# Three last stores of a filter-and-MLP kernel go through GpSimd's queue instead of SyncE's

## The chip, the cores and the metric

The kernel runs on one core of a Trainium2 chip. Its time is in device microseconds (us), taken over whole executions. One further execution was recorded by the hardware profiler, and its trace is what is read below. The engines are called PE (TensorE, matrix products), DVE (VectorE), ACT (ScalarE), POOL (GpSimd) and SP (SyncE). SP, ACT and POOL issue DMAs, each in the order of its own instruction queue.

## What is computed

The input `x` has 8 sequences of 3008 tokens with 256 features, in float32. Each feature is filtered along its sequence in the frequency domain, and then every token goes through two dense layers with a leaky ReLU between them:

```python
X = np.fft.rfft(x, axis=1)
Y = X * (filt_r + 1j * filt_i)[None, :, :]
y = np.fft.irfft(Y, n=3008, axis=1).reshape(8 * 3008, 256)
h = y @ w_in                       # 256 -> 2048
out = np.maximum(0.01 * h, h) @ w_out   # 2048 -> 256, float32
```

## The kernel before

The transform is done as small matrix products over 94 x 32 = 3008 positions, sequence by sequence. Its stages move data through DMAs on SP and end in `yt`, the filtered tokens. The last of POOL's work for it is the sum in L326 for the eighth sequence.

The dense layers run over 47 chunks of 512 tokens (`ci` = 0 to 46). For chunk `ci`, `moe1` (L516) multiplies by `w_in` into PSUM, and ACT writes the leaky ReLU into `gts[ci]` (L527). One chunk later the product with `w_out` follows. From chunk 3 on, it is made of seven half-size products, with sums on DVE before them (L563) and after them (L625 to L681). A chunk's result lies in two tiles, `rows(ci, 0)` and `rows(ci, 1)`, of two groups of 128 tokens each. `store` (L581) and `pieces` (L569) cut a group of 128 tokens into one or more DMAs, because output rows of different sub-sequences do not lie at one stride.

All steps are put on one list with a time (`at`, `soon`) and are emitted in the order of those times. So a delay given to `soon` only decides the place of an instruction in its engine's queue, and at run time each instruction waits for semaphores alone. Each DMA uses one of eight semaphores of its kind in turn, one set of eight for SP and ACT together and one for POOL.

After chunk 46's first layer, PE has only the products of chunk 46 left. They end in this order, each followed by its DVE instruction and its stores:

- `m2` (L639): DVE adds the left 128 columns of two token groups into `rows(46, 0)` (L641). These are the early half-width tiles, two DMAs of 128 tokens x 128 columns, through `store` (L583).
- the product with `wt[3]`, in two tiles, in `m4_tile` (L669): DVE writes L670 for each token group. The largest piece of group 0 is stored by SP and that of group 1 by ACT (L673). What is left of group 1, eight tokens of full width, is the leftover piece (L675).
- the last product, in two tiles, in `m3_tile` (L677): DVE writes L678, and the right 128 columns of each group are stored, group 0 by SP and group 1 by ACT (L583).

Behind its last instruction every engine has the program's end (all on L808): SP waits for every DMA semaphore in turn, each engine has a DRAIN, and POOL then waits until the others have reported, gives them leave, drains and clears semaphores, and a second such round ends the program.

Of the kernel before, what the change touches and what calls it, by code (L numbers as in the profile page):

```python
# [11 lines left out]
P = 128  # L12
# [65 lines left out]
def kernel(  # L78
# [9 lines left out]
    nc = tc.nc  # L88
# [83 lines left out]
    def at(time, f):  # L172
        clock["n"] += 1
        heapq.heappush(work, (time, clock["n"], f))
# [12 lines left out]
    def soon(delay, f):  # L187
        at(clock["now"] + delay, f)
# [356 lines left out]
    def sum_places(ci):  # L545
        return last_sums if ci == NCHUNK - 1 else [s1, quarter(ci, 1, 0), s2, s4]
# [8 lines left out]
    def quarter(ci, i, j):  # L555
        return gts[ci][:, ts(j, NCH), ts(token_half(ci, i), TH)]
# [12 lines left out]
    def pieces(ci, tj, of, d0=0, dn=D):  # L569

        t, end = ci * CH + tj * P, ci * CH + (tj + 1) * P
        lo = 0
        while t < end:
            e = min(end, (t // QT + 1) * QT)
            b, h = divmod(t // QT, N2 // 4)
            row = b * N + (t % QT) // 4 * N2 + 4 * h
            yield (bass.AP(tensor=out.tensor, offset=out.offset + row * D + d0,
                           ap=[[N2 * D, (e - t) // 4], [D, 4], [1, dn]]), of[lo : lo + e - t])
            lo, t = lo + e - t, e

    def store(*what, queue=nc.sync):  # L581
        for to, of in pieces(*what):
            queue.dma_start(to, of)  # L583

    def product(ci, a, w, after, last_sum=None, of=None, each=None):

        po = of
        if of is None:
            po = out_banks[done["products"] % 2][:, 0]
            done["products"] += 1  # L590
        if each is None:
            of = [po[:, t] for t in range(2)]

        def one(t, c):
            if last_sum is not None:
                need(("sum", ci, last_sum))
            nc.tensor.matmul(of[t], a()[:, c, ts(t, P)], w[:, c, :],  # L597
                             start=(c == 0), stop=(c == NCH - 1))
            if c < NCH - 1:
                return  # L600
            if each is not None:
                each(t, of[t])
            elif t == 1:
                after(po)
        return [lambda t=t, c=c: one(t, c) for t in range(2) for c in range(NCH)]

    def rows(ci, i):

        if (ci, i) not in osts:
            osts[ci, i] = outp.tile([P, 2, 3, P], FP32, tag="ost", name=f"ost_c{ci}_h{i}")  # L610
        return osts[ci, i]

    def stores(ci, i, of=range(2)):
        for j in of:
            store(ci, 2 * i + j, rows(ci, i)[:, j, 0:2, :].rearrange("p k d -> p (k d)"))

    def twice(po):
        ap = [list(v) for v in po.ap]
        return bass.AP(tensor=po.tensor, offset=po.offset, ap=[ap[0], ap[1], [0, 2], ap[2]])
# [3 lines left out]
    def last_product(ci):  # L623
        def after(po):
            add(rows(ci, 0)[:, :, 1], po, rows(ci, 1)[:, :, 2], AL.add)  # L625
            soon(AFTER[5], lambda: stores(ci, 0))
        return product(ci, lambda: sum_places(ci)[3], b22, after, 3)

    def products(ci):
        a11, a12, a21, a22 = (lambda i=i, j=j: quarter(ci, i, j) for i in range(2) for j in range(2))  # L630

        def after5(po):
            add(rows(ci, 1)[:, :, 1:3], twice(po), part[1], AL.add)
            soon(AFTER[5], lambda: stores(ci, 1))

        def m1():
            return product(ci, a11, b11, lambda po: nc.scalar.copy(t1, po))

        def m2(early=None):  # L639
            def after(po):  # L640
                add(rows(ci, 0)[:, :, 0], po, t1, AL.add)  # L641
                if early is not None:
                    soon(0.3, lambda: [store(ci, 2 + t, rows(ci, 0)[:, t, 0], 0, P) for t in range(2)])
            return product(ci, a12, b21, after)

        def m7():
            return product(ci, lambda: sum_places(ci)[1], wt[2], lambda po: add(v7, po, t1, AL.add), 1)

        def m6(of=None):
            return product(ci, lambda: sum_places(ci)[2], wt[1], lambda po: add(part[1], twice(po), part[0], AL.add), 2, of)  # L650

        if ci == NCHUNK - 1:
            free = [w[:, :CH].rearrange("p (a t d) -> p a t d", a=2, t=2)[:, 0] for w in wide + single]
            return last_product(ci - 1) + m1() + m7() + m2(ci) + m6(free[0]) + last_three(ci, free[1:])
        if ci > W0:
            items = m1() + last_product(ci - 1) + m2() + m7()
        else:
            done["products"] += 1
            items = m1() + [lambda: None] * (2 * NCH) + m2() + m7()
        items += m6()  # L660
        items += product(ci, a22, wt[3], lambda po: add(rows(ci, 1)[:, :, 0], po, u3, AL.add))
        return items + product(ci, lambda: sum_places(ci)[0], wt[0], after5, 0)

    def last_three(ci, free):

        free += [b[:, 0] for b in out_banks]
        low, high = rows(ci, 0), rows(ci, 1)

        def m4_tile(t, po):  # L669
            add(high[:, t, 0], po, u3[:, t], AL.add)  # L670
            parts = list(pieces(ci, t, high[:, t, 0:2, :].rearrange("p k d -> p (k d)")))
            parts.sort(key=lambda v: -v[1].shape[0])
            soon(0.02, lambda: (nc.sync, nc.scalar)[t].dma_start(*parts[0]))  # L673
            for v in parts[1:]:
                soon(0.6, lambda v=v: nc.sync.dma_start(*v))  # L675

        def m3_tile(t, po):  # L677
            add(low[:, t, 1], po, high[:, t, 2], AL.add)  # L678
            soon(0.02, lambda: store(ci, 2 + t, low[:, t, 1], P, P, queue=(nc.sync, nc.scalar)[t]))

        items = product(ci, lambda: sum_places(ci)[0], wt[0], lambda po: add(high[:, :, 1:3], twice(po), part[1], AL.add), 0, free[0])  # L681
        items += product(ci, lambda: quarter(ci, 1, 1), wt[3], None, of=[f[:, 0] for f in free[1:3]], each=m4_tile)
        return items + product(ci, lambda: sum_places(ci)[3], b22, None, 3, of=[f[:, 0] for f in free[3:5]], each=m3_tile)
# [63 lines left out]
    queue = [(time, n, *v) for n, (time, *v) in enumerate(groups)]  # L747
    heapq.heapify(queue)
    while queue:
        time, n, stage, b, g, f = heapq.heappop(queue)  # L750
        t = max(time, last + GAP)
# [61 lines left out]
```

## Time and profile before

| what | value |
|---|---|
| median of 3 runs (lowest to highest) | 745.34 us (744.58 to 745.47) |
| the profiled execution's own time | 744.82 us |
| its span, first to last instruction | 742.8 us |
| PE busy | 735.8 us (99%) |
| ACT busy | 559.8 us (75%) |
| DVE busy | 506.7 us (68%) |
| POOL busy | 167.6 us (23%) |
| start of POOL's last sum (L326) | 612.2 us |
| start of the last DVE instruction (L678) | 738.55 us |

The span is what the profiler sees between the first and the last instruction, and the execution's own time is 2.02 us more. Busy time of an engine is the time in which it works on an instruction. Issuing a DMA from SP or ACT, waiting for semaphores and draining are not counted as busy, so the program's end after 738.85 us shows only in single rows of the trace.

### The profile page before, as it was taken

How to read it: one execution, taken by the hardware profiler on the slowest of the kernel's cores; microseconds unless marked ns; L12 is line 12 of the kernel's file. 1: busy time of each engine (PE TensorE's matmuls, PEld its weight loads, DVE VectorE, ACT ScalarE, POOL GpSimd, SP SyncE). 2: the span in 40 equal slices, each digit the busy share in tenths (PEclk: the TensorE clock that was granted, in tenths of full speed). 3: DMA queues.
4: the chain of work that ended last, by engine and by line, in shares of the span. 5: the costliest groups of instructions: out<-in, count | busy, mean ns of one | idle time of the engine just before them, and what ended most of it. 6: DMA issues, size and time to landing. Idle time of an engine off the chain costs nothing.

```text
span 742.8 us, 18986 instructions
## 1 busy us (share of the span) xinstructions
PE 735.8 (99%) x7793; PEld 513.7 (69%) x7793; DVE 506.7 (68%) x690; ACT 559.8 (75%) x769; POOL 167.6 (23%) x171
## 2 busy tenths in 40 slices
PE   9999999999999999999999999999999999999997
PEld 3656667776777777777777777777777777777776
DVE  7987647776776766766777667766677676465566
ACT  4776797888878788877787787887777777777762
POOL 5503422332323212131232322121212210000000
PEclk9999999999999999999999999999999999999999
DMA  9997797888876666665676656544453343211012
GB/s 206 229 227 193 201 227 222 198 208 207 215 182 149 159 188 176 161 150 159 195 175 155 160 156 175 157 140 111 143 170 110 107 107 97 62 54 55 30 45 71
DMA packets 119879, 113.84 MB, mean 153 GB/s; under 512 B 16384, under 2 KB 93056, under 8 KB 119600
## 3 DMA queue, kind: packets, MB, share of 16 engines
q1 hardware_dynamic: 104457, 94.94, 43.9%
q0 software_dynamic: 15056, 17.50, 15.7%
q8 instruction: 61, 1.00, 0.6%
q10 hardware_dynamic: 279, 0.19, 0.1%
q14 instruction: 26, 0.21, 0.1%
HBM read 57.74 MB, written 50.33 MB: 145 GB/s over the span
## 4 chain that ended last, share of the span: by engine, by line
PE 98%; DVE 1%; ACT 0%; issue 0%; DVEq 0%; ACTq 0%
PE ph L524 44%; PE pf L597 18%; PE po_ps L597 18%; PE pf L262 3%; PE pf L358 3%; PE pf L311 2%; PE pf L333 2%; PE po_ps L380 2%; PE pf L689 1%; PE po_ps L689 1%; PE pf L432 0%; ACT yt L347 0%; PE pf L449 0%; PE ph L408 0%; DVE big L291 0%; DVE big L441 0%
## 5 line engine op out<-in xcount | busy, mean ns | idle before, releaser
L527 ACT ACTIVATE gt_c<-ph 128x1024 f16<-128x1024 f32 x376 | 385.6, 1026 | 131.6 <-PE ph L524 121.2
L524 PE MATMUL ph<-yt,w_in_sb 128*128 128x512 f16 x1504 | 446.9, 379 | 0.2 <-ACT yt L347 0.2
L597 PEld LDWEIGHTS <-gt_c 128*128 128x128 f16 x2800 | 203.3, 98 | 102.3
L326 POOL TENSOR_TENSOR y_b_g<-p_b_g,p_b_g 128x512 f16<-128x512 f32 x84 | 117.8, 1405 | 411.0 <-DMA p_b_g<-p_b_g 219.9
L597 PEld LDWEIGHTS <-big 128*128 128x128 f16 x2128 | 152.0, 98 | 69.2
L524 PEld LDWEIGHTS <-w_in_sb 128*128 128x128 f16 x1504 | 119.8, 98 | 12.9 <-DVE yt L347 0.4
L320 DVE TENSOR_TENSOR p_b_g<-pf,fb_sb 128x512 f32<-128x512 f32 x78 | 53.7, 688 | 31.4 <-PE pf L311 16.5
L597 PE MATMUL po_ps<-wt_sb,gt_c 128*128 128x128 f16 x704 | 70.0, 219 | 0.0
L597 PE MATMUL pf<-wt_sb,gt_c 128*128 128x128 f16 x688 | 68.5, 219 | 0.0
L597 PE MATMUL pf<-w_out_sb,gt_c 128*128 128x128 f16 x720 | 67.9, 219 | 0.0
L597 PE MATMUL pf<-wt_sb,big 128*128 128x128 f16 x704 | 67.2, 219 | 0.0
L597 PE MATMUL po_ps<-w_out_sb,gt_c 128*128 128x128 f16 x688 | 66.0, 219 | 0.0
L265 ACT CAST big<-pf 128x512 f16<-128x512 f32 x98 | 57.1, 588 | 11.7 <-PE pf L262 10.4
L597 PE MATMUL po_ps<-wt_sb,big 128*128 128x128 f16 x688 | 65.4, 219 | 0.0
L347 ACT CAST yt<-pf 128x376 f16<-128x376 f32 (+7 forms) x134 | 57.1, 441 | 10.0 <-PE pf L358 7.5
L563 DVE TENSOR_TENSOR big<-gt_c 128x2048 f16<-128x2048 f16 (+1 forms) x46 | 57.3, 1247 | 0.1
L323 DVE TENSOR_TENSOR p_b_g<-pf,fa_sb 128x512 f32<-128x512 f32 x84 | 57.2, 681 | 0.2
L563 DVE TENSOR_TENSOR big<-gt_c,big 128x2048 f16<-128x2048 f16 (+1 forms) x45 | 56.7, 1261 | 0.0
L563 DVE TENSOR_TENSOR gt_c<-gt_c 128x2048 f16<-128x2048 f16 x43 | 55.9, 1301 | 1.0
L563 DVE TENSOR_TENSOR big<-big,gt_c 128x2048 f16<-128x2048 f16 (+1 forms) x45 | 54.8, 1219 | 0.1
L335 ACT CAST big<-pf 128x512 f16<-128x512 f32 x84 | 49.0, 584 | 4.7 <-PE pf L333 2.7
L262 PE MATMUL pf<-x_sb,small_sb 128*128 128x512 f16 x109 | 41.3, 379 | 0.0
(98 smaller groups left out, 628.3 us busy)
## 6 DMA issues: line engine op xcount, KB each, us to landing
dz<-big SPq DMA_DIRECT2D x98, 256.0 KB
p_b_g<-p_b_g SPq DMA_DIRECT2D x156, 128.0 KB
out_dram<-ost_c_h SPq DMA_DIRECT2D x118, 128.0 KB
big<-dz SPq DMA_DIRECT2D x42, 256.0 KB
big<-dz SPq DMA_DIRECT2D x56, 192.0 KB
x_sb<-in_x_dram POOLq DMA_DIRECT2D x40, 192.0 KB, 4.4
x_sb<-in_x_dram POOLq DMA_DIRECT2D x2, 768.0 KB, 9.2
w_in_sb<-in_moe_w_in_dram POOLq DMA_DIRECT2D x1, 1024.0 KB, 13.7
```

The costliest lines, as they stand in the source:

```text
L262: nc.tensor.matmul(ps, fwd1, x_sb[:, ds(2 * g, 2), :], start=True, stop=True)
L265: copy(st[:, ds(2 * (g % 2), 2), :], ps)
L320: nc.vector.tensor_tensor(p2[:], ps, fb, AL.mult)
L323: nc.vector.tensor_tensor(p1[:], ps, fa, AL.mult)
L326: ("y", b, g), lambda: nc.gpsimd.tensor_tensor(y1[:], p1[:], p3[:], AL.add)))
L335: nc.scalar.copy(st2[h % 4][:, ds(2 * (g % 2), 2), :], ps)
L347: copy(yt[:, dt, ds(to, 4 * n)].rearrange("p (a c) -> p a c", c=4), v[:, ds(a, n)])
L358: nc.tensor.matmul(ps[:, j, :], z2[h % 4][:, j, ts(dt, P)], i1_sb[:, 4 * h + j, :N1], start=True, stop=True)
L524: nc.tensor.matmul(ph[:, j, :], w_in_sb[:, dt, ts(ct, P)], yt[:, dt, ds(ci * CH % RING, CH)], start=(dt == 0), stop=(dt == NDT - 1))
L527: nc.scalar.activation(gts[ci][:, ds(2 * g, 2), :], ph, AF.Lrelu)
L563: nc.vector.tensor_tensor(*(v[:, ds(c0, n)] for v in (o, i0, i1)), op)
L597: nc.tensor.matmul(of[t], a()[:, c, ts(t, P)], w[:, c, :], start=(c == 0), stop=(c == NCH - 1))
```

## The change

The three stores are issued by POOL (`nc.gpsimd`) instead of SP (`nc.sync`), with shorter delays: the two early half-width tiles after `m2`, and the leftover piece in `m4_tile`.

```diff
@@ m2(early) @@
                 add(rows(ci, 0)[:, :, 0], po, t1, AL.add)
                 if early is not None:
-                    soon(0.3, lambda: [store(ci, 2 + t, rows(ci, 0)[:, t, 0], 0, P) for t in range(2)])
+                    soon(0.05, lambda: [store(ci, 2 + t, rows(ci, 0)[:, t, 0], 0, P, queue=nc.gpsimd) for t in range(2)])
@@ m4_tile @@
             for v in parts[1:]:
-                soon(0.6, lambda v=v: nc.sync.dma_start(*v))
+                soon(0.02, lambda v=v: nc.gpsimd.dma_start(*v))
```

The order of instructions on PE, DVE and ACT is the same as before. SP loses the two early stores, which stood just ahead of its L673, and its very last DMA. Its queue then ends with chunk 45's stores, the large piece of group 0 (L673) and the right half of group 0 (L583). POOL's queue, which ended with the sum of L326, ends with the two early stores and the leftover piece, all three ahead of its DRAIN.

## The prediction

> **What bounds the kernel now.** I read the page's slices and its chain of waits first.
>
> ```profile
> PE   9999999999999999999999999999999999999997
> POOL 5503422332323212131232322121212210000000
> PE 98%; DVE 1%; ACT 0%; issue 0%; DVEq 0%; ACTq 0%
> ```
>
> PE is busy in all slices and carries 98% of the chain. The change touches no PE instruction, so nothing before the last slice can move. POOL has no work in the last seven slices. What counts is the stretch after PE's last product, so next come the timelines of DVE, ACT and SP from 735.85 us, a row being start, duration, engine.
>
> ```profile
> 737.37 0.58 DVE L670 TENSOR_TENSOR ost_c_h<-pf,big 128x128 f32<-128x128 f32 x2
> 738.55 0.29 DVE L678 TENSOR_TENSOR ost_c_h<-po_ps,ost_c_h 128x128 f32<-128x128 f32 x1 [0.15 <-PE po_ps L597]
> 737.98 1.49 ACTq L673 DMA_DIRECT2D out_dram<-ost_c_h  x1
> 739.58 0.63 ACTq L583 DMA_DIRECT2D out_dram<-ost_c_h  x1
> 735.90 0.54 SPq L583 DMA_DIRECT2D out_dram<-ost_c_h  x1
> 736.49 1.55 SPq L583 DMA_DIRECT2D out_dram<-ost_c_h  x1
> 738.13 0.55 SPq L673 DMA_DIRECT2D out_dram<-ost_c_h  x1
> 738.78 0.55 SPq L583 DMA_DIRECT2D out_dram<-ost_c_h  x1
> 739.38 0.70 SPq L675 DMA_DIRECT2D out_dram<-ost_c_h  x1
> ```
>
> The last data are ready at 738.85 (738.55 + 0.29), yet ACT issues their store only at 739.58, because its store before that took 1.49 us to issue. SP's second early store took 1.55 us and held L673, whose data were ready at 737.65, until 738.13. An undisturbed issue takes 0.54 to 0.55 us. The rows of the program's end (L808) show what waits for these stores: a view of that line, then of POOL around its first drain, then SP's waits.
>
> ```profile
> L808 POOLq EVENT_SEMAPHORE  x4: 17/17/17, 742.1 to 742.7; - x4
> L808 POOLq DRAIN  x3: 46/98/7785, 612.2 to 742.6; - x3
> ...
> L808 POOLq DRAIN  x1: 7785/7785/7785, 612.2 to 612.2; - x1
> 612.20 1.54 POOL L326 TENSOR_TENSOR y_b_g<-p_b_g,p_b_g 128x512 f16<-128x512 f32 x1 [4.60 <-PE ph L524]
> ...
> SPq L808 <- DMA out_dram<-ost_c_h: 1.2, 3, 0.6
> ```
>
> By the trace's semaphore records ACT's last store has landed at 741.80. SP's closing waits run on at 741.82, 741.88 and 741.94, POOL's wait for the other engines ends at 742.09, and the span ends 0.71 us later, at 742.80. The telling row is POOL's first DRAIN: 7.785 us, from 612.17 to 619.96. Its last sum ended at 613.74 (semaphore at 613.75), so the drain went on for 6.21 us with no sum left and no POOL DMA in flight. Nobody noticed, because everyone else came to the end 122 us later.
>
> **The change part by part.** *SP loses three issues.* The two early stores (0.54 + 1.55 us) and the leftover (0.70 us) leave its queue. L673 can then start when its data are there, at 737.70 instead of 738.13. ACT's store of group 1 still starts at 737.98, but beside SP's 0.55 us issue instead of beside the end of the stalled one. I take its end at 738.55 to 738.80 (0.55 us, or 0.55 us after SP's has ended at 738.25) instead of 739.48. ACT's last store then starts at about 738.93 instead of 739.58: 0.65 us earlier. If it lands the same 2.22 us after its start (741.80 - 739.58), the last landing is 741.15. The bounds are 738.90 + 1.90 = 740.80 (SP's first early store was in but for one late packet after 1.90 us), and no gain.
>
> *SP's closing waits* stand in a fixed order, one semaphore after another, 0.06 us apart when already met. The last hardware DMA falls on the third semaphore of the eight instead of the sixth, so three more waits follow its landing: + 0.18 us. Without anything else the end thus moves by -0.65 + 0.18 = -0.47 us.
>
> *POOL gets three issues.* It has had no work since 613.74, so they take no time from other work. The early stores wait for L641 (done at 735.87), the leftover for the second L670 (done at 737.95). The trace has no store issued by POOL. Its nearest rows are the loads of L199, 0.51 to 0.91 us each, and the load of L470 with 1.18 us. I take 0.54 us, the median of L199:
>
> ```profile
> L199 POOL DMA_DIRECT2D x_sb<-in_x_dram x61: 507/536/907, 1.2 to 428.7; - x61
> ...
> DMA to landing us min/median/max: 2.5/4.1/9.6
> ```
>
> The early stores are issued by 737.0, 0.9 us before the leftover's data, and the leftover by 738.00 + 0.54 = 738.54 (to 739.2 with 1.18). It lands 2.5 to 4.1 us after its start, at 740.5 to 742.1. Bytes are the same, 64, 64 and 8 KB. Nothing waits behind them on POOL except the end of the program.
>
> *And that is the price.* POOL's DRAIN now stands behind DMAs whose last one goes out at 738.5. POOL's four drains differ in one thing. The one at the program's start took 0.184 us and ended 0.05 us after POOL's last memset, with no DMA before it. The two at the very end took 0.098 and 0.046 us, with no DMA since the drain before. The long one followed 75 POOL DMAs (61 of L199, 8 of L207, and 6 single ones). So I read the 6.21 us as the drain's own work on those DMAs, 0.083 us each, though all had landed long before. With 78 it is 6.46 us. The bounds are 5.9 us (POOL's rows being rough) and, if the whole 7.785 us is its work, 8.10 us. A drain that need not work costs 0.05 us, which I keep as the first rival, since then the cover at 612 us still holds.
>
> The Trainium skill's page GPSIMD Engine Reference, section Instruction dispatch, offers another reading of such a tail: the first call of freshly loaded code on GpSimd loads it for about 6 us (5.95 measured there) with no row of its own. The tail of 6.21 us does not contradict it; by that fixed price the estimate would be 0.5 us lower, and no run here tells the two apart yet.
>
> *The sum.* The drain ends at 738.54 + 6.46 = 745.00, POOL's wait follows at 745.02 instead of 742.09, and the 0.71 us after it stay: + 2.93 us. All DMAs have landed by then, so the 0.47 us gained on SP and ACT are covered. The profiled execution would take 744.82 + 2.93 = 747.75 us. The runs' median is 0.52 us above that execution, so I predict 745.34 + 2.93 = 748.3 us. With the bounds, the drain ends at 744.4 to 746.7 (739.2 + 6.46 = 745.7 lies within), which gives 747.6 to 749.9 us.
>
> **The rivals.** *The drain does its work ahead (not slower).* Its row begins at 612.17, before the sum queued ahead of it has started (612.20), so POOL's sequencer runs ahead of the engine. In the changed kernel it may reach the drain at about 613 us, deal with the 75 landed DMAs then, and have only three left at 738.5: 3 x 0.083 = 0.25 us, over at about 738.8, or a little after the leftover's landing. Then the gain on ACT shows: 745.34 - 0.47 = 744.9 us, 744.5 to 745.4. It decides if the drain takes up finished DMAs before the engine is idle. For it speaks that early start; against it, that in 612.17 to 613.74 the drain either did no work or so little that 6.21 us were left. The Trainium skill's page DMA: Bandwidth & Descriptors, section Issuing engines are not separate DMA queues, says that issuing from several engines saves only the sequencer's issue time; alone that gives this rival's small gain, and the shortened issue of ACT is where the trace would bear it out.
>
> *POOL's last store lands last.* With no long drain, but the leftover landing at 742.1, SP's closing waits end at about 742.1 + 0.29 + 0.30 = 742.69 instead of 742.09 (from 741.80 to 742.09 took 0.29, and the semaphore of this store is waited for five places earlier): + 0.6 us, 745.9 us. For it speaks the 4.1 us median of POOL's loads; against it, that these are 192 KB and this store is 8 KB, where 2.5 us is nearer.
>
> *More is gained than I can place.* To be faster by 1.5 us the end would have to move by more than the 1.0 us between 741.80 and the bound of 740.80. Only something in front of PE's last product could do that, and no instruction there moves.
>
> **How the numbers follow.** The drain behind POOL's DMAs: 0.64, all slower. The drain working ahead: 0.26, and the late landing: 0.07, both within 0.2%, which is 1.5 us and about what a measurement of this kernel can tell from no change. The unplaced gain: 0.03. That makes faster 0.03, same 0.33, slower 0.64. The likeliest case's own range is 747.6 to 749.9. The range over the cases reaches down to 744.6 to take in most of the second, and up to 749.9.
>
> **What would show it.** Right: POOL's first DRAIN ends at about 745, 6 to 8 us after the issue of L675 on POOL, and POOL's waits of L808 start there instead of at 742.1. SP's closing waits are done before 742. ACT's issue of L673 takes 0.55 to 0.8 us and its L583 starts near 738.9. Wrong: a DRAIN that ends within 0.3 us of the leftover's issue or landing, with SP's last wait ending the chain. An ACT issue still at 1.5 us would show that SP's early stores were not what held it.

## The result, and the profile after

The changed kernel takes 749.80 us (median of 14 runs, 747.61 to 752.04), the kernel before 746.13 us beside it (14 runs, 744.58 to 749.56). The ratio is 1.0042, with a 95% interval of 1.0028 to 1.0056: about 3.1 us slower (0.0042 x 745.34). The two medians lie 3.7 us apart, a ratio of 1.0049; 1.0042 is estimated from all runs of both. The forecast was 2.93 us on 745.34, a ratio of 1.0039.

The profiled execution of the changed kernel took 750.18 us with a span of 748.3 us, 5.4 us more than the one of before. Not all of that is the change. The waits of PE between 105 and 113 us, in the kernel after:

```profile
PE pf L358 <- DMA big<-dz: 1.9, 1, 1.9
```

PE waited 1.9 us once for a transfer in the first sixth of the program. The profile of before has no wait of PE in this stretch, and nothing of the change lies there. PE comes out of this wait 2.18 us late (its L358 at 111.44 instead of 109.26 us) and stays so to the end. I therefore compare the two ends by what I call the tail, from the start of the last L678 to the end of the span: 742.828 - 738.554 = 4.27 us before, 748.252 - 740.739 = 7.51 us after. The change costs 3.24 us there. PE itself is no slower: it is busy 735.6 us after and 735.8 us before. In the traces of the kernels below the last DVE instruction starts anywhere from 738.3 to 741.4 us, so what happens ahead of the tail differs from trace to trace by about as much as the change costs. Below, "+1.0" is a time in us after the start of the last L678 of the same kernel, because this instruction is where the kernels' ends can be laid over each other.

The page's slices and its chain, after:

```profile
PE   8999989999999999999999999999999999999995
POOL 5503411332223212131242322121112120000000
PE 93%; DMA 4%; ACT 1%; DVE 1%; issue 0%; POOL 0%; ACTq 0%; POOLq 0%
```

PE's last slice fell from 7 to 5 tenths: its products end earlier in that slice, since more follows them. POOL still shows zeros in the last seven slices: draining is not counted as busy, and its three issues of 1.76 us in all are less than a tenth of a slice of 18.7 us. The chain's 4% of DMA are transfers ahead of 111.4 us, which it reaches through the wait there. POOLq is a new member of it, and the page gives it no visible share. So the page hardly tells where the time went. The timelines of DVE, POOL, ACT and SP around the end, after (start, duration, engine):

```profile
739.56 0.58 DVE L670 TENSOR_TENSOR ost_c_h<-pf,big 128x128 f32<-128x128 f32 x2
740.74 0.29 DVE L678 TENSOR_TENSOR ost_c_h<-po_ps,ost_c_h 128x128 f32<-128x128 f32 x1 [0.15 <-PE po_ps L597]
738.36 1.16 POOL L583 DMA_DIRECT2D out_dram<-ost_c_h  x2 [122.43 <-DVE ost_c_h L641]
740.43 0.59 POOL L675 DMA_DIRECT2D out_dram<-ost_c_h  x1 [0.91 <-DVE ost_c_h L670]
740.17 1.75 ACTq L673 DMA_DIRECT2D out_dram<-ost_c_h  x1
742.01 0.62 ACTq L583 DMA_DIRECT2D out_dram<-ost_c_h  x1
739.87 0.54 SPq L673 DMA_DIRECT2D out_dram<-ost_c_h  x1
740.61 0.54 SPq L583 DMA_DIRECT2D out_dram<-ost_c_h  x1
```

SP's two stores start as soon as their data are there, and take 0.54 us each. ACT's L673 takes 1.75 us, not less than the 1.49 us of before but more. The program's end (L808), and then the waits of SP from 735 us on, after:

```profile
L808 POOLq EVENT_SEMAPHORE  x4: 17/17/17, 747.5 to 748.1; - x4
L808 POOLq DRAIN  x3: 46/102/7057, 740.4 to 748.0; - x3
```

```profile
SPq L808 <- PEq L808: 3.7, 2, 3.2
SPq L808 <- DMA out_dram<-ost_c_h: 2.7, 2, 1.9
```

POOL's long DRAIN now starts at 740.41 and takes 7.057 us, so it ends at 747.47. POOL's first closing wait follows at 747.5, where before it stood at 742.1. SP's waits for DMAs are over at +3.58, and then SP waits 3.2 us for the leave that POOL gives after its DRAIN. The view names PE, whose own DRAIN had long ended. All transfers had landed 3.5 us before POOL's DRAIN ended (the last one at +3.26, the DRAIN at +6.73).

### The profile page after: what moved, and what is told of

It reads as the page before. It is cut to its first block, busy times and chain, and to the rows that moved or that the text cites. A ratio compares the mean times of both kernels' runs of the same rounds, so it can differ in the third digit from the quotient of the medians.

```text
span 748.3 us, 18987 instructions
## 1 busy us (share of the span) xinstructions
PE 735.6 (98%) x7793; PEld 513.6 (69%) x7793; DVE 506.6 (68%) x690; ACT 559.7 (75%) x769; POOL 168.9 (23%) x174
## 3 DMA queue, kind: packets, MB, share of 16 engines
q0 software_dynamic: 15152, 17.64, 15.8%
## 4 chain that ended last, share of the span: by engine, by line
PE 93%; DMA 4%; ACT 1%; DVE 1%; issue 0%; POOL 0%; ACTq 0%; POOLq 0%
PE ph L524 43%; PE pf L597 18%; PE po_ps L597 18%; PE pf L262 3%; PE pf L358 3%; PE pf L311 2%; PE pf L333 2%; PE pf L689 1%; PE po_ps L689 1%; DMA f_sb<-fwd_const 1%; DMA x_sb<-in_x_dram 1%; DMA dz<-big 1%; PE pf L432 0%; DMA big<-dz 0%; ACT yt L347 0%
## 5 line engine op out<-in xcount | busy, mean ns | idle before, releaser
L326 POOL TENSOR_TENSOR y_b_g<-p_b_g,p_b_g 128x512 f16<-128x512 f32 x84 | 117.4, 1399 | 411.5 <-DMA p_b_g<-p_b_g 241.3
```

The source lines that it names most:

```text
L326: ("y", b, g), lambda: nc.gpsimd.tensor_tensor(y1[:], p1[:], p3[:], AL.add)))
```

## The experiments

In the diffs, unchanged lines are left out. The profile shows when the leftover's issue on POOL ends, and the prediction counts 0.083 us per DMA from there. The twelve kernels are grouped by question: which part of the change costs, what the DRAIN's time is, and what holds ACT's store.

**Which part.** Only the early stores on POOL, against the changed kernel:

```diff
-                soon(0.02, lambda v=v: nc.gpsimd.dma_start(*v))
+                soon(0.6, lambda v=v: nc.sync.dma_start(*v))
```

> Only the first half of the change: the two early stores go through GpSimd, the leftover piece stays on SP as before. Theory 1: the last drain follows the second early store, whose issue in the changed kernel ended 1.2 us before the start of the last DVE instruction, and works on 77 DMAs, 6.4 us: it ends 5.15 us after that start, and the tail is 5.9 us, 1.7 us longer than before and 1.6 us shorter than with the whole change. Theory 3 (5.3 us from the last landing, which for the second early store is 0.3 us after that start): tail 6.3 us. If moving stores to GpSimd cost only by the leftover: 4.25 us.

Only the leftover on POOL:

```diff
-  soon(0.05, lambda: [store(ci, 2 + t, rows(ci, 0)[:, t, 0], 0, P, queue=nc.gpsimd) for t in range(2)])
+  soon(0.3, lambda: [store(ci, 2 + t, rows(ci, 0)[:, t, 0], 0, P) for t in range(2)])
```

> Only the second half of the change: the leftover piece goes through GpSimd, the two early stores stay on SP. The tail is the time from the start of the last DVE instruction (L678) to the end of the span: 4.25 us before, 7.5 us with the whole change. Theory 1 (0.083 us for each of now 76 GpSimd DMAs, 6.3 us, from the end of the leftover's issue on, 0.27 us after that start): tail 7.3 to 7.4 us, so the one DMA of 8 KB costs nearly all of the change. If the price went with the bytes or the number of the moved stores: a third of 3.25 us, tail 5.3 us.

The shorter delays alone, with all three stores on SP:

```diff
-  soon(0.05, lambda: [store(ci, 2 + t, rows(ci, 0)[:, t, 0], 0, P, queue=nc.gpsimd) for t in range(2)])
+  soon(0.05, lambda: [store(ci, 2 + t, rows(ci, 0)[:, t, 0], 0, P) for t in range(2)])
-                soon(0.02, lambda v=v: nc.gpsimd.dma_start(*v))
+                soon(0.02, lambda v=v: nc.sync.dma_start(*v))
```

> Only the delays of the change, all three stores still on SP: the leftover piece then stands ahead of the right half of group 0 in SP's queue. Theory: the shorter delays carry none of the loss; the right half is issued up to 0.7 us later than before, and ACT's last store still ends the program: tail 4.2 to 4.5 us. Rival: the order of stores on SP matters, and the tail grows by the whole 0.7 us to 4.9 us or more.

The drains at the program's end of these three kernels, one view each:

```profile
L808 POOLq DRAIN  x3: 46/102/7067, 736.8 to 744.3; - x3
```

```profile
L808 POOLq DRAIN  x3: 46/102/6922, 738.0 to 745.4; - x3
```

```profile
L808 POOLq DRAIN  x3: 46/102/7767, 615.0 to 745.2; - x3
```

With the early stores alone the DRAIN starts 1.6 us earlier in the tail than with all three and ends at +5.14, which is 6.36 us after the second early store's issue; the tail is 5.93 us. With the leftover alone it ends at +6.59, 6.28 us after the leftover's issue; the tail is 7.38 us. So the one store of 8 KB costs 3.1 of the 3.24 us, and the two early ones, issued 1.5 us earlier, would cost 1.65 us by themselves. They do not add up, since there is one DRAIN and it starts behind the last. With the delays alone the long DRAIN stays at 615 us and the tail is 4.06 us, 0.21 us shorter than before and below the 4.2 to 4.5 us expected: the delays do not cost, the queue does.

**What the DRAIN's time is.** The changed kernel with one more DRAIN, right behind POOL's last sum, where POOL has 122 us to spare:

```diff
+    at(SL * NCHUNK, lambda: nc.gpsimd.drain())
```

> The changed kernel with one more DRAIN on GpSimd, right behind its last sum, where GpSimd then idles for over 120 us. The tail is the time from the start of the last DVE instruction (L678) to the end of the span: 4.25 us before, 7.5 us in the changed kernel. Theory 1 (a drain works 0.083 us for each GpSimd DMA that no earlier drain has dealt with): the added drain runs some 6.2 us past the last sum, at no cost; the last drain has 3 DMAs left, 0.25 us, and ends within 0.3 us of the leftover's issue, or 0.1 us after its landing if it waits for that, at most 1.6 us after the start of L678. SP's closing waits then end the program: tail 4.4 to 4.5 us, time within 0.1% of the kernel before. Theory 2 (a drain behind GpSimd DMAs loads code once, about 6 us): the same, but the last drain has no work of its own left. Theory 3 (the drain takes about 5.3 us from the landing of the last store on): tail 7.5 us as in the changed kernel, 0.4% slower than before.

The added drain (L780), then the program's end (L809), of this kernel:

```profile
L780 POOLq DRAIN  x1: 7797/7797/7797, 613.6 to 613.6; - x1
...
L809 POOLq DRAIN  x3: 51/102/1970, 739.6 to 744.2; - x3
```

The added drain does the work of the 75 earlier DMAs where nobody waits: 6.22 us past the end of the sum. The closing one now takes 1.970 us and ends at +1.64, 0.17 us after the leftover has landed (+1.47). In the two other kernels below with this early drain it ends 0.17 us after that landing as well. SP's waits for DMAs end the tail again, at 4.49 us. The time over all runs is 745.52 us (12 runs) against 745.48 us for the kernel before (17 runs), a ratio of 1.0001 with an interval of 0.9990 to 1.0013. The interval of the changed kernel lies wholly above that. Of its loss, 3.02 us of tail (7.51 - 4.49) is this drain.

The same drain in the midst of the program, behind 51 of the DMAs, so that 27 are left for the end:

```diff
+    at(119, lambda: nc.gpsimd.drain())
```

> The changed kernel with one more DRAIN on GpSimd between the fourth and the fifth sequence's sums, 51 DMAs before it and 27 behind it. Theory 1: the added drain takes about 4.2 us, and the last one 27 x 0.083 = 2.2 us behind the issue of the leftover, which ends about 2.5 us after the start of the last DVE instruction, before SP's closing waits do: tail 4.4 to 4.5 us. Theory 2 (code loaded once): the added drain takes about 6 us, the last one under 0.2 us behind the leftover's issue. Theory 3: the last drain again 6.4 us behind the issue, tail 7.5 us.

The added drain (L780) and the program's end (L809), here:

```profile
L780 POOLq DRAIN  x1: 6017/6017/6017, 269.2 to 269.2; - x1
...
L809 POOLq DRAIN  x3: 51/102/2949, 740.4 to 744.9; - x3
```

The sum ahead of the added drain ends at 270.93, the drain at 275.19: 4.26 us for 51 DMAs, 0.0835 us each. The closing one ends 2.34 us after the leftover's issue, for 27 DMAs, where 27 x 0.083 = 2.24. The price goes with the number of DMAs since the drain before. It does not go with their size: by the DMA queues of this trace, POOL's queue moved 13136 packets and 14.39 MB before 269.2 us, ahead of the added drain, and 2016 packets and 3.25 MB after it. By packets or bytes the second drain would have cost under a fourth of the first; it cost 0.55 of it, and 27 is 0.53 of 51. Two prices that differ are also what a fixed price cannot give, neither one for code loaded the first time nor one that runs from the last landing. The reading by the page GPSIMD Engine Reference, section Instruction dispatch, of the Trainium skill falls with it: by that, one of the two drains would have paid about 6 us and the other next to nothing.

Then the other direction, and here every theory put on record for it failed. The changed kernel with forty more small loads on POOL (L782), spread from 465 to 609 us:

```diff
+    extra = cpool.tile([P, 40, 16], FP16, name="extra")
+    for k in range(40):
+        at(225 + 2 * k, lambda k=k: nc.gpsimd.dma_start(extra[:, k], small_d.ap()[:, 0, 0:16]))
```

> The changed kernel with 40 more GpSimd DMAs of 32 bytes per partition into a tile that nobody reads, spread between the sums of the seventh and eighth sequence, landed long before the end. Theory 1 (0.083 us for each DMA): the drain goes on for 118 x 0.083 = 9.8 us behind the issue of the leftover instead of 6.45, and the tail is 10.8 us instead of 7.5. Theory 2 (code loaded once) and theory 3 (5.3 us from the last landing): 6.4 us and a tail of 7.5 us.

The program's end (L811), here:

```profile
L811 POOLq DRAIN  x3: 46/98/4198, 738.9 to 743.6; - x3
```

With 118 DMAs behind it the drain is shorter than with 78, and ends 3.59 us after the leftover's issue. That is close to 43 x 0.083 = 3.57, the forty and the three stores. I took it that POOL had let go of the first 75 when it issued the later ones, and made three kernels to learn by what rule. Twenty instead of forty:

```diff
-    extra = cpool.tile([P, 40, 16], FP16, name="extra")
-    for k in range(40):
-        at(225 + 2 * k, lambda k=k: nc.gpsimd.dma_start(extra[:, k], small_d.ap()[:, 0, 0:16]))
+    extra = cpool.tile([P, 20, 16], FP16, name="extra")
+    for k in range(20):
+        at(225 + 4 * k, lambda k=k: nc.gpsimd.dma_start(extra[:, k], small_d.ap()[:, 0, 0:16]))
```

> The changed kernel with twenty more small GpSimd DMAs (98 in all), spread over the time in which the forty stood. With forty the closing drain ended only 3.59 us after the leftover's issue, 43 x 0.083: the first 75 DMAs no longer counted. Three theories for why. R, by kind: the added DMAs themselves, or when they come, make POOL let go of all that came before; then 23 x 0.083 = 1.9 us after the leftover's issue. C, by count: POOL keeps a bounded number of DMAs, over 78 and below 118, and lets go at the bound; then 98 x 0.083 = 8.1 us if the bound is over 98, about 1.9 to 3.6 us if it is below. D, by size: POOL's queue keeps a bounded number of packets. The changed kernel's 78 DMAs had 15152 packets there, 947 on each of 16 engines, and the one with forty 16432, 1027 on each, so the bound would lie between; here it is 987, and so 8.1 us if the bound is above that, which I take as likelier.

Forty of one partition each:

```diff
-        at(225 + 2 * k, lambda k=k: nc.gpsimd.dma_start(extra[:, k], small_d.ap()[:, 0, 0:16]))
+        at(225 + 2 * k, lambda k=k: nc.gpsimd.dma_start(extra[0:1, k], small_d.ap()[0:1, 0, 0:16]))
```

> The changed kernel with forty more GpSimd DMAs at the same places as before, each of one partition (32 bytes) instead of 128: 118 DMAs in all, but with hardly more packets on POOL's queue than the changed kernel has. R and C: as with the forty of 128 partitions, the drain ends about 3.6 us after the leftover's issue. D: the queue's bound is not reached, nothing is let go of, and the drain ends 118 x 0.083 = 9.8 us after it; the stretch from the last sum's start to the end is then about 10.9 us.

Ten of four pieces per partition (a piece is one unbroken run of bytes):

```diff
-    extra = cpool.tile([P, 40, 16], FP16, name="extra")
-    for k in range(40):
-        at(225 + 2 * k, lambda k=k: nc.gpsimd.dma_start(extra[:, k], small_d.ap()[:, 0, 0:16]))
+    extra = cpool.tile([P, 10, 4, 16], FP16, name="extra")
+    for k in range(10):
+        at(225 + 8 * k, lambda k=k: nc.gpsimd.dma_start(extra[:, k], small_d.ap()[:, 0:4, 0:16]))
```

> The changed kernel with ten more GpSimd DMAs, each of 128 partitions by four pieces of 32 bytes: 88 DMAs in all, and as many added packets as the forty had, if packets go by pieces. R: 13 x 0.083 = 1.1 us after the leftover's issue (so about the leftover's landing). C: 88 x 0.083 = 7.3 us, unless the bound lies between 78 and 88. D: the bound is passed and the first DMAs are let go of: 1.1 us, or as much as 13 DMAs and those not yet let go of take, below 4 us. With the one of forty thin DMAs this tells D from R and C; the one with twenty tells R from C.

The program's end (L811) with twenty, with forty thin and with ten wide loads, one view each:

```profile
L811 POOLq DRAIN  x3: 46/98/2755, 738.3 to 742.8; - x3
```

```profile
L811 POOLq DRAIN  x3: 46/108/2453, 740.0 to 744.5; - x3
```

```profile
L811 POOLq DRAIN  x3: 46/98/2551, 739.0 to 743.5; - x3
```

| added loads | DMAs in all | packets on POOL's queue | drain's end after the leftover's issue |
|---|---|---|---|
| none | 78 | 15152 | 6.45 us |
| 40 of 128 pieces | 118 | 16432 | 3.59 us |
| 20 of 128 pieces | 98 | 15792 | 2.14 us |
| 40 of one partition, 16 pieces | 118 | 16432 | 1.86 us |
| 10 of 512 pieces | 88 | 15472 | 1.94 us |

None of my three rules fits all four. That the added loads clear whatever came before them (R) gives 1.9 us for twenty (2.14 measured) and 3.6 for forty (3.59), but 3.6 for the thin ones (1.86) and 1.1 for the wide ones (1.94). One bound on the number of DMAs (C) asks for the same price for both sets of forty. The bound on packets (D) could not be tried as meant, because the thin loads made as many packets as the full ones (in the trace each is 16 pieces of 2 bytes and not one of 32) and the wide ones fewer; still it gives 8.1 us or 1.9 for twenty, and the same time for both sets of forty. What stands is that in all four kernels loads issued by POOL from 464 us on took a good part of the old work off the closing drain, and that no row shows where it went: no drain stands between, the added loads take 0.48 to 0.81 us each to issue, and POOL's sums after 440 us take 35 to 36 us together in these kernels as in the changed one. Nor is R saved by a price that goes with a load's pieces: with 0.083 us for each of the three stores, a load of 512 pieces would have to cost 0.17 us (an estimate from the drain with the wide loads), and the eight loads of L207, of 768 pieces each in the trace, stand ahead of the midway drain, which took 0.0835 us per DMA. By what rule the old work goes is open. The price of 0.083 us per DMA holds in this case where nothing was issued by POOL between the burst of loads that ends at 431 us and the end, and in the kernel with the drain midway.

**What holds ACT's store.** The prediction had ACT's issue of 1.49 us down to SP's stalled store beside it, and it did not get shorter. First guess: ACT's first DMA is slow. The kernel before, with one small early load on ACT:

```diff
+    warmed = cpool.tile([P, 16], FP16, name="warmed")
+    nc.scalar.dma_start(warmed[:], small_d.ap()[:, 0, 0:16])
```

> The kernel before with one DMA more on ACT at the start, 32 bytes per partition into a tile that nobody reads. ACT's issue of L673 took 1.49 us before and 1.75 us in the changed kernel, and is ACT's first DMA. Theory A (a first DMA of an engine costs it 0.65 to 0.9 us more): L673 takes about 0.85 us, as SP's stores of 26 and 28 times 4 tokens do, ACT's last store starts about 0.65 us earlier, and the tail is 3.6 us instead of 4.25. Theory B (ACT's issue waits for SP's issues of the same moment): 1.5 us and a tail of 4.25 us as before.

The changed kernel with this load and the early drain, to see if both together bring a gain:

```diff
+    warmed = cpool.tile([P, 16], FP16, name="warmed")
+    nc.scalar.dma_start(warmed[:], small_d.ap()[:, 0, 0:16])
...
+    at(SL * NCHUNK, lambda: nc.gpsimd.drain())
```

> The changed kernel with one more DRAIN on GpSimd behind its last sum and one small early DMA on ACT. If a drain ahead takes the price of the change away and a first DMA on ACT is slow (theory A): tail 3.6 to 3.9 us, 0.4 to 0.65 us under the kernel before, 0.05% to 0.09%, below what its runs can tell. If ACT's issue waits for SP's (theory B): tail 4.4 to 4.5 us.

ACT's timeline at the end, of the first and of the second (L675 is what L673 was, two lines further down):

```profile
738.85 1.51 ACTq L675 DMA_DIRECT2D out_dram<-ost_c_h  x1
```

```profile
738.48 1.75 ACTq L675 DMA_DIRECT2D out_dram<-ost_c_h  x1
```

The early load changed nothing: 1.51 and 1.75 us, as without it, and tails of 4.30 and 4.42 us. The second kernel took 745.66 us (12 runs) against 745.11 us (17 runs), ratio 1.0008, interval 0.9993 to 1.0023. In all kernels here but the next one, ACT's issue is 1.49 to 1.51 us where the early stores are on SP and 1.75 to 1.76 us where they are on POOL. So moving them made it longer by 0.25 us. SP's stall is not what holds it either: with the shorter delays alone SP's second early store takes 0.59 us instead of 1.55, and ACT's issue still takes 1.50 us. ACT's first store has 4 x 30 pieces, its second one 4 x 32, as SP's have. To tell the shape from the engine, the kernel with the early drain and the two groups' stores exchanged:

```diff
-            soon(0.02, lambda: (nc.sync, nc.scalar)[t].dma_start(*parts[0]))
+            soon(0.02, lambda: (nc.scalar, nc.sync)[t].dma_start(*parts[0]))
...
-            soon(0.02, lambda: store(ci, 2 + t, low[:, t, 1], P, P, queue=(nc.sync, nc.scalar)[t]))
+            soon(0.02, lambda: store(ci, 2 + t, low[:, t, 1], P, P, queue=(nc.scalar, nc.sync)[t]))
```

> The changed kernel with an early drain on GpSimd, and with ACT's and SP's last stores exchanged: ACT now stores the groups of 4 x 32 pieces and SP those of 4 x 30. ACT's issue of the 4 x 30 store took 1.75 us with the early drain, SP's of 4 x 32 took 0.54. If the shape makes it long, SP's issue of the 4 x 30 store is now 1.5 us or more and ACT's 0.6. If it is ACT's first issue after a long time without one, ACT's first store still takes 1.5 us or more and SP's stays below 0.9. If neither is long, it was the meeting of both, and the last landing comes 0.6 us or more earlier; the time would then be 0.5 us below that of the kernel with the drain alone.

The timelines of ACT and SP at its end:

```profile
740.10 0.66 ACTq L673 DMA_DIRECT2D out_dram<-ost_c_h  x1
740.86 0.55 ACTq L583 DMA_DIRECT2D out_dram<-ost_c_h  x1
740.40 0.88 SPq L673 DMA_DIRECT2D out_dram<-ost_c_h  x1
741.38 0.55 SPq L583 DMA_DIRECT2D out_dram<-ost_c_h  x1
```

Now neither is long: ACT's 4 x 32 takes 0.66 us and SP's 4 x 30 takes 0.88. The shape has a part in it: SP's seven earlier 4 x 30 stores in the kernel before took 0.92 to 1.01 us each, where an undisturbed 4 x 32 took 0.54. But the shape by itself does not make 1.5 us, nor does ACT's first issue by itself. The long one in the changed kernel was ACT with the 4 x 30 store, begun 0.30 us after SP's; the exchange undid all of that at once, and which of it made the issue slow stays open. The last landing comes at +2.54 instead of +3.27 (the kernel with the early drain), and the tail is 3.76 us: 0.73 us shorter than there and 0.51 us shorter than before the change. This is the version with the shortest end of all. The exchange without the move to POOL was not tried, so it is not shown that the shorter end needs POOL at all. Its one execution took 746.69 us, against 744.95 us for one of the kernel before; that difference arose ahead of the tail, since its last L678 starts at 740.97 us, where 738.55 was before. A gain of 0.5 us in 745 is 0.07%, below what these runs can tell, so it is shown in the trace alone.

## Why the prediction was right

*Nothing moves before PE's last product.* Right: the 2.18 us at 111 us are a wait for a load that the change doesn't touch, and the tail holds the rest.

*The price of the DRAIN.* Right in size and in kind, for this kernel. Forecast was 78 x 0.0828 = 6.46 us after the leftover's issue; measured 6.45. The drains of the kernels that keep the order of POOL's loads lie on one line: 27 DMAs 2.34 us, 51 DMAs 4.26, 75 DMAs 6.22, 76 DMAs 6.28, 77 DMAs 6.36, 78 DMAs 6.45 (all from the end of POOL's last issue or sum). The reason in the text, that the drain works on each DMA since the last drain, is borne out by the drain midway. It is not the whole rule: added loads from 464 us on lowered the price instead of raising it.

*The rivals.* "The drain does its work ahead" falls: the DRAIN's row starts at 740.41, 0.02 us before the leftover's issue, and the work of all 78 DMAs follows that issue. The row begins some 0.02 to 0.03 us ahead of the start of the instruction before it in both kernels (0.15 us with the early stores alone), and the early start that the prediction took for a sign (612.17) means no more than that. The page DMA: Bandwidth & Descriptors of the Trainium skill, section Issuing engines are not separate DMA queues, promised only the issue time as a gain; the trace shows the issue time saved on SP, whose L673 starts 0.03 us after its data instead of 0.48, and a price on POOL that the section does not have. "POOL's last store lands last" falls too: the leftover landed at +1.46, 1.8 us before ACT's last store.

*ACT's store.* Wrong. The step that failed is "I take its end at 738.55 to 738.80 ... instead of 739.48" and with it the gain of 0.65 us: the issue grew from 1.49 to 1.75 us, and ACT's last store landed at +3.26 instead of +3.25. As the prediction said of that case, SP's early stores were not what held it. The 0.55 us was SP's for a 4 x 32 store; ACT's is a 4 x 30 store, for which the trace of before had 0.92 to 1.01 us on SP. SP's waits for DMAs, to be done before 742 us, were over at 744.3, or 742.1 without the 2.18 us, for the same reason. Exchanging the two groups' stores brought it down, and nothing else that I tried. This did not touch the forecast, because the drain ended after all of it. In the first rival, which counted on it, it would have: with the drain out of the way the tail is 4.49 us, 0.22 us more than before, not 0.47 us less.

*SP's closing waits.* Right: after the last landing they take 0.32 us (+3.26 to +3.58), and before 0.13 us (+3.25 to +3.38), so 0.19 us more where 0.18 was forecast. POOL's wait in the kernel with the early drain ends 0.21 us later than before (+3.75 against +3.54).

*The sum.* Forecast 2.93 us, measured 3.24 in the profiled tails. The mis-sized term is the issue of the leftover. POOL took it up 0.29 us after its data were ready (740.43 against 740.14, the end of L670's second instruction), where I allowed 0.05, and issued in 0.59 us instead of 0.54. With 0.05 us more behind the drain (0.79 us from its end to the span's end, 0.73 forecast), less 0.01 for the drain itself, that makes 0.33 us; the 0.02 to 0.03 us too much is the span's end of before, 742.83, which the prediction has as 742.80. The prediction's own bounds for the drain's end, 744.4 and 746.7, give 747.7 and 750.0 us and not 747.6 and 749.9. The measured median of 749.80 lies so near the upper end partly because the kernel before came out at 746.13 us beside it, 0.79 us above the median that the prediction added to; the mechanism has no share in that.

## What to carry to other kernels

In this kernel a DMA on GpSimd late in the program was paid for in the DRAIN at the program's end, and the price was 0.083 us for each DMA that GpSimd had issued since its last drain, not for the one store that was moved: an 8 KB store cost 3.1 us. (Small loads issued on GpSimd in between lowered it, by a rule that is open.) Before moving a last store to another queue, look for the DRAIN rows of that engine, where they stand now and what has to come before them after the edit. If such a store must go through GpSimd, a drain in a stretch where GpSimd is idle takes the old work out of the end, as it did here (1.0001 instead of 1.0042), but also then nothing was won over SP's queue.

## What was not expected of the hardware

GpSimd's closing drain gets shorter, not longer, when more small loads are issued late: 6.45 us with 78 DMAs, 1.86 to 3.59 us with 88 to 118. The same store of 4 x 30 pieces took 1.75 us to issue on ACT behind SP's, and 0.88 us on SP behind ACT's. SP's second early store took 1.55 us to issue in the kernel before and 0.59 us in the kernel with the shorter delays alone, though it starts 2.07 us ahead of the last L678 in both; what held it was not tried.
